# Moving one attention unit's key and query transposes from TensorE to DMA transposes, with a later second half of a weight load

## The chip, the cores and the metric

The kernel runs on one core of a Trainium2 chip. The metric is device time in microseconds (us). Three runs of the kernel before the change gave 590.16 us as their median, with 588.65 as the lowest and 591.14 as the highest. One further execution was taken with the hardware profiler; it is the one that the page and the trace tell of.

## The reference

An attention layer with normalised queries and keys, followed by a two-layer MLP with a residual. The sizes are batch 8, 12 heads, 448 positions and 64 values per head; the model width is 768 and the hidden width 3072. All inputs and the output are float32.

```python
q_n, k_n = rmsnorm(q, g_q), rmsnorm(k, g_k)            # over the 64 values of a head
scores = (1 / sqrt(64)) * matmul(q_n, k_n.transpose(0, 1, 3, 2))
attn = softmax(scores, axis=-1)
x = matmul(attn, v)                                    # (8, 12, 448, 64), then heads joined: (8, 448, 768)
xn = (x - mean(x)) / sqrt(var(x) + 1e-6) * g_ln        # over the 768 values of a row
out = x + relu(xn @ w_ch1) @ w_ch2                     # 768 -> 3072 -> 768
```

## The kernel before, in words

**Units and pairs.** The heads are taken two at a time: a pair `p` is two heads of one batch, and there are 48 pairs, six to a batch. A unit `u` is what is loaded and normalised at once: unit 4 and all later ones hold two pairs. Pairs 10 and 11 are unit 6 (the end of batch 1), pairs 12 and 13 are unit 7 (the start of batch 2), pairs 14 and 15 are unit 8, pairs 16 and 17 unit 9.

**Preparing a unit** (`pieces`). Each piece has a letter: `b` begin, `a` and `c` the squares of keys and queries (ScalarE, L254), `d` and `e` the sums of these squares (VectorE, L257), `g` the root (ScalarE, L260 and L261), `i` the product of the keys with the two gains (POOL, L271), `j` the high half of the keys in float16 (ScalarE, L279), `k` their low half, a difference (VectorE, L282), `l` the scaled queries (VectorE, L79), `m` the second copy of the queries (VectorE, L318), `z` the values, and `x`, `y`, `Y` the transposes by DMA.

**Two ways to transpose.** Scores need keys and queries with the 64 (twice 64) values on the partitions. For units below `DMA_UNIT`, TensorE transposes them against an identity matrix: `trans_k` and `trans_q` issue seven matmuls each for a pair into the PSUM bank `tr` (L360, L363, L374, L377), and VectorE copies each result to SBUF (L365, L382). From `DMA_UNIT` on, SP issues six DMA transposes for a unit (L298, L304 three times, L310 twice), straight from SBUF to SBUF; the queries are then scaled in four pieces instead of one, so that they lie in the order that these transfers want; and the values come by five cast-on-the-way DMAs that POOL issues (L212, L215) instead of a staging load and three casts on POOL (L324, L330). Keys go to `kU[0]` or `kU[1]`, queries to `qU[0]` or `qU[1]`: the DMA units use buffer `u % 2`, the TensorE units one fixed buffer, `PE_SET`.

**Banks for scores.** Scores go to two PSUM banks in turn. From the pair after the first DMA unit's first pair on, the bank `tr` is free of transposes and serves as a third one (`score_bank`).

**The order of the work.** Every engine's instruction order is the order in which the program emits them; nothing is reordered by a planner. Batch 0's attention follows a list written by hand (`ORDER`). From then on, the MLP of batch `b` is emitted in chunks, and attention steps of the following batches are put between the chunks (`run_rest`). A step is numbered `7 p + i`: the scores of pair `p`, block `i`, and the product with the values for pair `p - 1`. `EARLY` and `TRANS_AT` say at which steps the pieces of units 5 to 9 are emitted; later units follow `PLAN`. `TAIL[b]` is the number of chunks at the end of batch `b`'s MLP that have no attention step beside them: with `TAIL[0] = 11`, the steps of pairs 6 to 12 are spread over the first 34 of batch 0's 45 chunks.

**The MLP of batch 0** (`first_mlp`). It has 21 chunks of the first layer (L702, PSUM tile `psH`; three more blocks were done earlier) and 24 of the second (L712, `psC`). A chunk is six matmuls. The first 12 of these 24 chunks use the first 384 columns of W2, the last 12 the other 384. From batch 1 on, the second layer works on sums and differences of W2's quarters, which VectorE forms once (`weight_sums`, L745): its twelve differences are emitted among the last nine chunks of batch 0 and the first of batch 1, and need both halves of W2.

**W2's load** (`load_w2`, L600). POOL issues it in two halves, each one DMA that reads float32 and writes 128 x 24 x 384 float16. Half 0 is emitted at step 47, half 1 at step 61, in each case behind that step's pieces, which include `i`, the key product on POOL. A matmul that reads a half waits for the whole transfer.

**SP's queue** carries the loads of queries and keys, the DMA transposes and most stores, in program order; `RING` says at which pieces the loads of later units are emitted.

Of the kernel before, what the change touches and what calls it, by code (L numbers as in the profile page):

```python
# [22 lines left out]
UNITS = [(0, 0, 1), (0, 2, 1), (0, 4, 2), (0, 8, 2)]  # L23
# [20 lines left out]
V5.3 V5.4 V5.5 Q6 a5 i5 V5.6 T3 T4 S6.0 S6.1 S6.2 S6.3 T5 S6.4 A V6.0 V6.1 N0 V6.2 N1 V6.3  # L44
S6.5 S6.6 d5 V6.4 X0 X1 U0 N2 R Q7 X2 c5 e5 j5 g5 k5 l5 z5 U1 U2 V6.5 M m5 V6.6 L7 L8k K7
""".split()
DMA_UNIT = 8
PE_SET = (DMA_UNIT + 1) % 2
EARLY = {5: (42, 49), 6: (47, 56), 7: (61, 69), 8: (75, 83), 9: (89, 97)}
TRANS_AT = {8: (84, 85, 86), 9: (100, 102, 104)}  # L50
PLAN = ((0, "bai"), (1, "dc"), (3, "j"), (5, "k"), (6, "e"), (7, "g"), (8, "l"), (9, "m"),
        (12, "z"), (15, "x"), (16, "y"), (18, "Y"))
LOAD_AT = 3, 1
# [7 lines left out]
RS_RATIO = 4.0  # L61
HALF, HCOL = NFF // 2, DM // 2
DOWN = 10
TAIL = (11, 13, 17, 13, 17, 13, 19, 0)
FLAG_AT = (6, 30)
E_RING = 9
RING = [(u, n) for u in (4, 6, *range(DMA_UNIT, len(UNITS))) for n in "kq"]


def _rsqrt(nc, out, a, t, eps, mul=1.0):  # L70
# [5 lines left out]
def _scaled(nc, out, x, r):  # L76

    g = x.shape[1]
    nc.vector.scalar_tensor_tensor(  # L79
        out=out, in0=x, scalar=8.0,  # L80
        in1=r.unsqueeze(2).broadcast_to([x.shape[0], g, D]), op0=ALU.mult, op1=ALU.mult)
# [6 lines left out]
class _Fast:  # L88
# [95 lines left out]
    def load_unit(self, u, which=(1, 0, 2)):  # L184
        nc = self.nc
        b, hs, m = UNITS[u]
        eng = nc.sync
        hS = self.hS.rearrange("p f n -> p (f n)").bitcast(FP32)
        home = {(4, 2): (hS, 0), (5, 0): (hS, 1920), (5, 1): (hS, 2816), (5, 2): (hS, 3712),
                (6, 2): (self.free, 3840), (7, 0): (self.free, 0), (7, 1): (self.free, 896),  # L190
                (7, 2): (self.free, 1792)}
        t = self.loads.setdefault(u, [None] * 3)
        for n in which:
            if (u, n) in home:
                x, c = home[u, n]
                t[n] = x[:, c:c + 896].rearrange("p (g d) -> p g d", d=D)
            else:
                t[n] = self.p_in.tile([128, 14, D], FP32, tag="kq", name="qk"[n])
            self.load_main(eng, n, t[n][:, 0:6 * m], b, hs, 2 * m)
            self.load_left(eng, n, t[n][:, 6 * m:7 * m], b, hs, 2 * m,  # L200
                           nc.gpsimd if (u, n) == (DMA_UNIT + 1, 1) else None)

    def load_v(self, u):

# [24 lines left out]
    def pieces(self, u):  # L229
# [55 lines left out]
        def qn():  # L285
            if u < DMA_UNIT:
                _scaled(nc, c["qn"][:, :, 0], c["t"][0], c["r", 0])
                return
            x, r = c["t"][0], c["r", 0]
            x3, r3 = (y[:, 0:12].rearrange("p (h j) d -> p h j d", j=3) for y in (x, r.unsqueeze(2)))  # L290
            for j in range(3):
                _scaled(nc, c["qn"][:, 4 * j:4 * j + 4, 0], x3[:, :, j], r3[:, :, j, 0])
            _scaled(nc, c["qn"][:, 12:14, 0], x[:, 12:14], r[:, 12:14])
# [47 lines left out]
        def values():  # L341
            if u >= DMA_UNIT:
                self.load_v(u)
            elif u == 0:
                vall()
            else:
                vmain()
                vleft()
# [70 lines left out]
    def score_bank(self, p):  # L419
        self.n_scores += 1  # L420
        if p > UNIT_PAIR[DMA_UNIT] and self.n_scores % 3 == 2:
            return self.ps_tr.tile([128, 512], FP32, tag="tr", name="psS3")
# [106 lines left out]
    def attention(self):  # L529

        n, nu, nb0, done = B * NPAIR, len(UNITS), NPAIR, set(ORDER)
        todo = {}
        for u in range(4, nu):
            p, m = UNIT_PAIR[u], UNITS[u][2]
            if u == 4:
                continue
            plan = [(7 * (p - 4) + x, y) for x, y in PLAN]
            if u in EARLY:
                st, e = EARLY[u]
                names = ["bai", "d", "c", "e", "j", "gz", "k", "l", "m"]  # L540
                if u > DMA_UNIT:
                    names = ["bai", "d", "c", "j", "k", "e", "gz", "l", "m"]
                plan = [(st + (e - st) * x // 9, y) for x, y in enumerate(names)]
                if u >= DMA_UNIT:
                    plan += zip(TRANS_AT[u], "xyY")
            for at, names in plan:
                if self.late_v(u):
                    names = names.replace("z", "")
                todo.setdefault(at, []).extend(
                    self.prep_ops(u)[y] for y in names if y + str(u) not in done)  # L550
                for y in set(names) & set("kl"):
                    i = RING.index((u, "qk"[y == "k"])) + 3 if u != 5 and u != 7 else nu * 2
                    if i < len(RING):
                        todo.setdefault(at + (LOAD_AT[y == "l"] if u not in EARLY else 1), []).append(
                            lambda x=RING[i]: self.load_unit(x[0], ("qk".index(x[1]),)))
                if u in (6, 7) and "b" in names:
                    todo[at].append(lambda u=u: self.load_w2(u - 6))
        steps, mark = [], [0]

        for p in range(nb0, n + 1):  # L560
            for i in range(7):
                c = []
                if i == 0 and p < n and p % NPAIR == 0 and p > nb0:
                    c.append(lambda b=p // NPAIR: self.batch(b))
                c += todo.pop(7 * p + i, [])
                if p < n and f"S{p}.{i}" not in done and i < 6:
                    c.append(lambda p=p, i=i: self.scores(p, i))
                if p > nb0:
                    for x in {0: (), 1: (0, 1)}.get(i, (i,)):
                        if f"V{p - 1}.{x}" not in done:  # L570
                            c.append(lambda p=p, x=x: self.values(p - 1, x))
                if p < n and i == 6 and f"S{p}.6" not in done:
                    c.append(lambda p=p: self.scores(p, 6))
                if p > nb0 + 1 and i == 1 and (p - 1) % NPAIR:
                    c.append(lambda p=p: self.stats(p - 2))
                if p + 1 < UNIT_PAIR[DMA_UNIT]:
                    if i == 2 and f"K{p + 1}" not in done:
                        c.append(lambda p=p: self.trans_k(p + 1))
                    if i == 4 and f"Q{p + 1}" not in done:
                        c.append(lambda p=p: self.trans_q(p + 1))  # L580
                if p > nb0 and p % NPAIR == 0 and i == 6:
                    c.append(lambda p=p: self.stats(p - 1))
                if c:
                    steps.append(c)
            if p > nb0 and p % NPAIR == 0:
                mark.append(len(steps))
        return steps, mark
# [369 lines left out]
    def run_rest(self):  # L957
        steps, mark, upto = self.steps, self.mark, self.upto
        for b in range(B):
            tail = TAIL[b]  # L960
            chunks = list(self.mlp_chunks(b))
# [267 lines left out]
```

## Time and profile before

| What | Value |
|---|---|
| Median of three runs | 590.16 us |
| Profiled execution, its own time | 588.15 us |
| Span of the profile | 586.6 us |
| TensorE busy | 557.1 us (95%) |
| VectorE busy | 381.9 us (65%) |
| ScalarE busy | 378.7 us (65%) |
| POOL busy | 174.9 us (30%) |
| Mean granted TensorE clock | 0.998 |

The profile is one execution. Its engines are PE (TensorE matmuls), PEld (TensorE weight loads, which lie beside the matmuls), DVE (VectorE), ACT (ScalarE), POOL (GpSimd) and SP, which only issues DMAs. A line such as `98.50 1.14 PE L712 MATMUL psC<-w,hS 128*128 128x384 f16 x6` gives the start, the duration of the group to its last end, the engine, the line of the kernel, the operation, what it writes and reads, the shape and the count. Matmuls overlap each other, so the time that one takes from the next is read from the starts. A bracket at the end gives the engine's idle time ahead of the instruction and what ended it. In the rows of queues, q0 is the queue that POOL's DMAs use and q1 the one of SP; the columns are packets, MB and the time of these packets as a share of 16 engines, which can pass 100%. A row of DMA issues ends with the size and the time from issue to landing. Line numbers are those of the kernel before; in the changed kernel, lines below the constants stand three further down.

### The profile page before, as it was taken

The page shows a single profiled execution, that of the slowest core. Times are in us where ns is not written, and L with a number is a line of the kernel's source. Part 1 is how long each engine was busy: PE and PEld are TensorE (multiplying, and loading weights), DVE is VectorE, ACT ScalarE, POOL GpSimd, SP SyncE. Part 2 cuts the span into 40 slices and gives each one's busy share as a digit, 9 for nine tenths or more (in the row PEclk, how much of TensorE's full clock was granted, in tenths as well). Part 3 has the DMA queues.
Part 4 walks back from the last instruction along what each step waited for, and adds up shares of the span by engine and source line. Part 5 has one row for each costly group of instructions (what it writes and reads, how often), then busy time and mean ns, then how long its engine had stood idle before and what let it go on. Part 6 is the DMA issues. An engine that isn't in the chain of part 4 may idle for free.

```text
span 586.6 us, 13477 instructions
## 1 busy us (share of the span) xinstructions
PE 557.1 (95%) x5366; PEld 407.3 (69%) x5366; DVE 381.9 (65%) x832; ACT 378.7 (65%) x693; POOL 174.9 (30%) x196
## 2 busy tenths in 40 slices
PE   3777999999999999999999999999999999999995
PEld 1555566677677768777687768777787777777773
DVE  5898666699667586855757576854757744663434
ACT  5996887438786588647787489737787477323130
POOL 2854333303241520653141421643141400020000
PEclk9999999999999999999999999999999999999999
DMA  7999998948672796967753697958843480030201
GB/s 209 285 221 236 197 197 115 145 124 124 138 100 58 181 128 131 138 158 116 130 92 57 181 134 132 131 149 124 137 60 64 126 104 1 3 107 2 82 0 58
DMA packets 172664, 71.43 MB, mean 122 GB/s; under 512 B 132548, under 2 KB 167556, under 8 KB 172596
## 3 DMA queue, kind: packets, MB, share of 16 engines
q1 hardware_dynamic: 130100, 51.60, 41.8%
q0 software_dynamic: 41552, 18.29, 24.1%
q8 instruction: 43, 0.70, 0.5%
q10 hardware_dynamic: 944, 0.62, 0.4%
q14 instruction: 25, 0.20, 0.1%
HBM read 52.30 MB, written 11.01 MB: 108 GB/s over the span
## 4 chain that ended last, share of the span: by engine, by line
PE 78%; DVE 8%; ACT 3%; DMA 2%; issue 1%; SPq 0%; DVEq 0%; ACTq 0%
PE psH L779 30%; PE psP L802 28%; PE psS L397 7%; PE oA L450 4%; PE psH L702 3%; PE psC L712 2%; PE oB L452 2%; PE psS L403 1%; DVE w2s L745 1%; DMA q<-in_q_dram 1%; ACT E L413 1%; DVE stat L625 1%; DVE khl L282 1%; DVE ssq L257 1%; DVE x L467 1%
## 5 line engine op out<-in xcount | busy, mean ns | idle before, releaser
L413 ACT ACTIVATE E<-psS,rr_all 128x448 f16<-128x448 f32 x336 | 202.9, 634 | 41.3 <-PE psS L397 36.2
L779 PE MATMUL psH<-xnT,w 128*128 128x256 f16 (+1 forms) x2016 | 225.8, 261 | 0.0
L779 PEld LDWEIGHTS <-w 128*128 128x128 f16 x2016 | 172.7, 98 | 24.0 <-issue 4.8
L782 ACT ACTIVATE hS<-psH 128x512 f16<-128x512 f32 x150 | 90.0, 600 | 96.5 <-PE psH L779 92.1
L802 PEld LDWEIGHTS <-hS 128*128 128x128 f16 x1080 | 100.0, 98 | 57.5 <-issue 1.1
L802 PE MATMUL psP<-w,hS 128*128 128x384 f16 x672 | 126.8, 326 | 0.0
L397 PE MATMUL psS<-qU,kU 128*128 128x448 f16 x288 | 102.0, 356 | 9.4 <-ACT E L413 6.0
L450 PEld LDWEIGHTS <-E 128*128 128x128 f16 x1008 | 70.6, 98 | 37.2 <-issue 4.8
L271 POOL TENSOR_TENSOR k<-k,gprod 128x896 f32<-128x896 f32 x19 | 40.4, 2128 | 166.6 <-ACT khl L254 139.0
L785 DVE TENSOR_TENSOR hS<-hS 128x512 f16<-128x512 f16 (+1 forms) x119 | 56.8, 484 | 22.3 <-ACT hS L782 20.8
L802 PE MATMUL psP<-w2s,hS 128*128 128x384 f16 (+1 forms) x408 | 69.9, 321 | 0.0
L450 PE MATMUL oA<-v,E 128*128 128x65 f16 x864 | 66.7, 193 | 0.4 <-DVE x L467 0.4
L739 DVE SCALAR_TENSOR_TENSOR x<-psP,rs_all,x 128x384 f32<-128x384 f32 x60 | 36.4, 617 | 41.9 <-PE psP L802 41.2
L452 PE MATMUL oB<-v,E 128*128 128x65 f16 x288 | 51.8, 193 | 0.3
L813 POOL TENSOR_TENSOR x<-x,hS 128x384 f32<-128x384 f32 x21 | 23.4, 1127 | 84.4 <-ACT hS L881 83.8
L212 POOL DMA_DIRECT2D v<-in_v_dram x51 | 39.1, 781 | 8.9 <-PE oB L452 8.0
L397 PEld LDWEIGHTS <-kU 128*128 128x128 f16 x288 | 28.1, 98 | 16.8 <-issue 6.0
L465 DVE RECIPROCAL rec_all<-oA 128x6 f32<-128x6 f32 x48 | 9.2, 191 | 46.8 <-PE oA L450 46.7
L282 DVE TENSOR_TENSOR khl<-k,khl 128x896 f16<-128x896 f32 x19 | 20.7, 1091 | 25.9 <-ACT khl L279 25.9
L881 ACT ACTIVATE hS<-hS,rs_all 128x384 f32<-128x384 f32 x27 | 14.6, 604 | 33.1 <-DVE hS L785 33.1
L452 PEld LDWEIGHTS <-E 128*128 128x128 f16 x336 | 32.5, 97 | 0.4 <-DVE xl L472 0.4
L257 DVE TENSOR_REDUCE ssq<-khl 128x14 f32<-128x896 f32 (+1 forms) x24 | 25.5, 1062 | 6.0 <-ACT khl L254 5.0
(136 smaller groups left out, 601.0 us busy)
## 6 DMA issues: line engine op xcount, KB each, us to landing
k<-in_k_dram SPq DMA_DIRECT2D x19, 384.0 KB, 3.9
q<-in_q_dram SPq DMA_DIRECT2D x19, 384.0 KB, 4.2
out_dram<-x SPq DMA_DIRECT2D x14, 384.0 KB, 3.0
w<-in_moe_w_ch_dram POOLq DMA_DIRECT2D x3, 1536.0 KB, 15.0
w<-in_moe_w_ch_dram POOLq DMA_DIRECT2D x2, 2304.0 KB, 19.5
out_dram<-x POOLq DMA_DIRECT2D x9, 384.0 KB, 3.0
v<-in_v_dram POOLq DMA_DIRECT2D x51, 64.0 KB, 4.2
qU<-qn SPq DMA_TRANSPOSE x85, 2.5
```

Of the source, the lines that this page charges most:

```text
L212: nc.gpsimd.dma_start(out[:, :, j, 0:D], main[:, :, j])
L257: nc.vector.tensor_reduce(out=c["ssq"][:, n], in_=c["sq", n], axis=AX.X, op=ALU.add)
L271: (nc.vector if u in DVE_KG else nc.gpsimd).tensor_tensor(out=c["t"][1], in0=c["t"][1], in1=sh.gprod.unsqueeze(1).broadcast_to([128, g, D] ...
L397: nc.tensor.matmul(ps[0][:, 0:S], c["main"][:, ts(i, 128)], c["q"][:, ts(h, S)], start=True, stop=True)
L413: nc.scalar.activation(out=o, in_=x[:, 0:S], func=AFT.Exp, scale=self.units[u][3][:, g:g + 1], bias=EXP_BIAS)
L450: nc.tensor.matmul(oA[:, t, cs], E[:, ts(t, 128)], rhs, start=(i == 0 and t == 0), stop=(i == 6 and t == 2))
L452: nc.tensor.matmul(oB[:, cs], E[:, 320:448], rhs, start=(i == 0), stop=(i == 6))
L739: self.nc.vector.scalar_tensor_tensor(out=x, in0=ps, scalar=self.rs[:, b, t:t + 1], in1=x, op0=ALU.mult, op1=ALU.add)
L779: nc.tensor.matmul(ps[:, i], sh.w1[:, dc, ts(f + i, 128)], self.xnT[:, dc, 256 - N:256], start=(i == 0 and dc == 0), stop=(i == k - 1 and ...
L782: nc.scalar.activation(out=hT[:, f:f + k], in_=ps, func=AFT.Relu)
L785: nc.vector.tensor_tensor(out=out, in0=a, in1=c, op=op)
L802: nc.tensor.matmul(bank[x][:, c], a[:, f], w[:, f, c], start=(start and f == 0), stop=(stop and f == HALF - 1))
```

## The change

- `DMA_UNIT` goes from 8 to 7: unit 7's keys and queries are transposed by six DMAs on SP at steps 70, 71 and 73, no longer by 28 matmuls of TensorE and four copies of VectorE; its query scaling is in four pieces, and its values come by five DMAs that POOL issues. The staging load of these values is still issued on SP, though nothing reads it.
- As consequences of that constant, `PE_SET` becomes buffer 0, so the TensorE units (0 to 6) use `kU[0]` and `qU[0]`, unit 7 uses buffer 1, and unit 8 buffer 0 behind unit 6; the third score bank is used from pair 13 on instead of pair 15. `RING`, and the load of unit 9 of which POOL issues a part, are written with their old numbers, so they stay.
- The second half of W2 is issued at step 75 instead of step 61, behind unit 8's key product on POOL. The first half stays at step 47.
- Unit 8's pieces between steps 79 and 80 change places: the low half of its keys comes one place sooner and its root one later. Against unit 9's order, which the constant would give it, its query sum stands sooner.
- `TAIL[0]` goes from 11 to 13: the attention steps of pairs 6 to 12 are spread over 32 chunks.

```diff
-DMA_UNIT = 8
+DMA_UNIT = 7
 PE_SET = (DMA_UNIT + 1) % 2
 EARLY = {5: (42, 49), 6: (47, 56), 7: (61, 69), 8: (75, 83), 9: (89, 97)}
-TRANS_AT = {8: (84, 85, 86), 9: (100, 102, 104)}
+TRANS_AT = {7: (70, 71, 73), 8: (84, 85, 86), 9: (100, 102, 104)}
+NAMES = {8: ["bai", "d", "c", "e", "j", "k", "gz", "l", "m"],
+         9: ["bai", "d", "c", "j", "k", "e", "gz", "l", "m"]}
+W2_AT = 47, 75
...
-TAIL = (11, 13, 17, 13, 17, 13, 19, 0)
+TAIL = (13, 13, 17, 13, 17, 13, 19, 0)
...
-RING = [(u, n) for u in (4, 6, *range(DMA_UNIT, len(UNITS))) for n in "kq"]
+RING = [(u, n) for u in (4, 6, *range(8, len(UNITS))) for n in "kq"]
...
-                           nc.gpsimd if (u, n) == (DMA_UNIT + 1, 1) else None)
+                           nc.gpsimd if (u, n) == (9, 1) else None)
...
                 names = ["bai", "d", "c", "e", "j", "gz", "k", "l", "m"]
-                if u > DMA_UNIT:
-                    names = ["bai", "d", "c", "j", "k", "e", "gz", "l", "m"]
+                if u > 7:
+                    names = NAMES[u]
                 plan = [(st + (e - st) * x // 9, y) for x, y in enumerate(names)]
...
-                if u in (6, 7) and "b" in names:
-                    todo[at].append(lambda u=u: self.load_w2(u - 6))
+        for g, at in enumerate(W2_AT):
+            todo.setdefault(at, []).append(lambda g=g: self.load_w2(g))
```

## The prediction

> **What bounds the kernel now.** I read the page's first part, then the windows, then TensorE's order of time.
>
> ```profile
> span 586.6 us, 13477 instructions
> PE 557.1 (95%) x5366; PEld 407.3 (69%) x5366; DVE 381.9 (65%) x832; ACT 378.7 (65%) x693; POOL 174.9 (30%) x196
> ```
> ```profile
> 60.00:80.00 20.00, 18.12 (x155) 11.51 (x156) 11.46 (x19) 17.42 (x35) 8.63 (x8) 1.00 1.08 200
> 80.00:100.00 20.00, 19.69 (x194) 12.93 (x193) 13.85 (x30) 16.52 (x34) 7.23 (x10) 1.00 1.06 147
> 100.00:110.00 10.00, 10.00 (x101) 6.79 (x100) 5.60 (x14) 5.40 (x9) 0.00 (x0) 1.00 0.90 153
> 110.00:120.00 10.00, 10.00 (x70) 5.94 (x68) 9.74 (x23) 3.31 (x7) 5.54 (x6) 1.00 0.87 136
> 120.00:130.00 10.00, 10.00 (x97) 7.89 (x96) 9.93 (x15) 4.09 (x7) 0.00 (x0) 1.00 0.26 88
> 130.00:140.00 10.00, 9.57 (x96) 7.25 (x93) 9.88 (x18) 7.93 (x15) 2.38 (x2) 1.00 0.72 144
> ```
>
> The columns are the stretch, its length, the busy time of PE, PEld, DVE, ACT and POOL, the granted clock, the DMA share and GB/s. From 100 to 130 us TensorE has no idle time, so here each instruction taken from it is worth its whole interval, and each wait put into it costs its whole length. This is the stage that the change edits: first MLP of batch 0, beside the attention of batch 1.
>
> ```profile
> 91.44 0.35 PE L397 MATMUL psS<-qU,kU 128*128 128x448 f16 x1
> ...
> 98.11 0.22 PE L360 MATMUL tr<-id,khl 128*128 128x128 f16 x1
> 98.16 0.50 PE L363 MATMUL tr<-id,khl 128*128 128x128 f16 x6
> 98.50 1.14 PE L712 MATMUL psC<-w,hS 128*128 128x384 f16 x6
> ...
> 108.81 0.22 PE L374 MATMUL tr<-id,qn 128*128 128x128 f16 x1
> ...
> 109.20 1.14 PE L712 MATMUL psC<-w,hS 128*128 128x384 f16 x6
> ...
> 111.80 10.90 PE L712 MATMUL psC<-w,hS 128*128 128x384 f16 x66
> 122.53 1.47 PE L779 MATMUL psH<-xnT,w 128*128 128x256 f16 x12
> ```
>
> The last 66 matmuls of the stage take 122.53 - 111.80 = 10.73 us, 0.163 us each. A chunk of six takes 0.98 us, and the 12 chunks that use the second half of W2 take 72 x 0.163 = 11.7 us. They are the last of the stage's 45.
>
> **The change, part by part.**
>
> *Transposes off TensorE.* The four groups of seven for pairs 12 and 13 go: 28 matmuls. A group holds TensorE from 98.11 to 98.50 and from 108.81 to 109.20, 0.39 us, so 4 x 0.39 = 1.56 us are gained at most. All four lie ahead of the first use of W2's second half. VectorE loses their four copies and gets unit 7's query scaling in four pieces:
>
> ```profile
> 98.92 0.64 DVE L365 COPY kU<-tr 128x960 f16<-128x960 f16 x1
> ...
> 100.47 1.29 DVE L79 SCALAR_TENSOR_TENSOR qn<-q,rr_all 128x256 f16<-128x256 f32 x4
> 101.68 0.62 DVE L382 COPY qU<-tr 128x896 f16<-128x896 f16 x1
> ```
> ```profile
> 83.21 1.09 DVE L79 SCALAR_TENSOR_TENSOR qn<-w2s,rr_all 128x896 f16<-128x896 f32 x1
> ```
>
> That is 2 x (0.64 + 0.62) = 2.5 us less, and 1.29 - 1.09 = 0.2 us more. No TensorE wait in 100 to 130 us hangs on VectorE; at most the 0.43 us of idle time in 130 to 140 us goes. I take nothing.
>
> *Transposes on SP's queue.* Unit 7 gets six transfers like unit 8's:
>
> ```profile
> 68.84 0.61 SPq L150 DMA_DIRECT2D k<-in_k_dram  x1
> 100.58 0.39 SPq L142 DMA_DIRECT2D q<-in_q_dram  x1
> ...
> 104.27 2.00 SPq L298 DMA_TRANSPOSE kU<-khl  x1
> ...
> 111.53 2.52 SPq L310 DMA_TRANSPOSE qU<-qn  x2
> ```
>
> ```profile
> 103.94 0.35 PE L397 MATMUL psS<-qU,kU 128*128 128x448 f16 x1
> ```
>
> Unit 8's last from 104.27 to 114.05, 9.8 us. Unit 7's query is scaled by 84.3, so they end near 94. Pair 12's first score stands at 103.94 (the third ahead of pair 13's keys); it comes two chunks and two groups sooner, 103.94 - 1.95 - 0.78 = 101.2. So 7 us are to spare, and SP has nothing else between 69.45 and 100.58. They cost nothing; with that cover gone the scores would wait for them, up to 9.8 us. Unit 8's own transposes now write the buffers that pair 11's scores read, but they are issued at about 103, some 3 us after those scores.
>
> *Values by transfer.* On POOL the two casts of unit 7 go and five issues come, as unit 8 has them (95.48, three in 2.30 us). POOL is idle from the end of those casts to 93.44, so this hides; pair 12's values are used only after its scores. Unit 8's key difference one place sooner, and its root one later, move among VectorE and ScalarE work with no TensorE wait behind it: nothing. A third score bank from pair 13 on is worth nothing either, since between 100 and 130 us TensorE waits for no bank; at most it shares the 0.43 us named.
>
> *Attention packed into 32 chunks instead of 34.* ScalarE's 16.52 us in 80 to 100 becomes 16.52 x 34 / 32 = 17.6 of 20, still below full. It may add some tenths of waiting ahead of W2's first use; by the next part such a wait lies beside the transfer and costs nothing.
>
> *The second half of W2, from step 61 to step 75.* This sets my forecast.
>
> ```profile
> 78.88 1.46 POOL L600 DMA_DIRECT2D w<-in_moe_w_ch_dram  x1
> ...
> 93.44 2.08 POOL L271 TENSOR_TENSOR k<-k,gprod 128x896 f32<-128x896 f32 x1 [11.69 <-issue]
> 95.48 2.30 POOL L212 DMA_DIRECT2D v<-in_v_dram  x3
> ```
> ```profile
> w<-in_moe_w_ch_dram POOLq DMA_DIRECT2D x1, 2304.0 KB, 17.7
> ```
>
> The row of 17.7 us is the second half: from 78.88 it lands at 96.6, and it is needed at 122.53 - 11.7 = 110.8. In the changed order POOL issues it behind unit 8's key product (93.44 to 95.48), where the value loads stand now. That product waits for ScalarE's square at step 75, behind the score at 91.44. The square's place moves 1.5 chunks up (by a count in both kernels' instruction orders 22 chunks stand ahead of that score now, 20.5 then): 1.5 x 0.98 = 1.46 us sooner. So it is issued at 95.48 - 1.46 = 94.0. Its first use moves 1.56 us up: 122.53 - 1.56 - 11.7 = 109.3. That leaves 15.3 us, less than either half takes now:
>
> ```profile
> w<-in_moe_w_ch_dram POOLq DMA_DIRECT2D x1, 2304.0 KB, 21.2
> ```
>
> This is the first half, issued at 61.98 beside SP's loads. How fast it moves in company and alone is in the queues' packets, for 70 to 79 us and for 88 to 94 us:
>
> ```profile
> q0 software_dynamic: 1487, 1.14, 80.7%
> q1 hardware_dynamic: 1439, 0.86, 43.0%
> ```
> ```profile
> q0 software_dynamic: 1531, 1.17, 125.5%
> ```
>
> That is 165 packets per us beside SP's loads and 255 alone. A half is 3072 rows, so 12.0 us alone and 18.6 in company. In the new place SP's queue is busy again, with two loads and unit 8's transposes from about 100 on (rows above):
>
> ```profile
> q1 hardware_dynamic: 5448, 1.90, 66.6%
> ```
>
> These are its packets from 100 to 116 us, 341 per us against 160 in the company above. Lower end: 12.0 us alone and 2.7 us, what a small value load takes to land in this window:
>
> ```profile
> v<-in_v_dram POOLq DMA_DIRECT2D x1, 64.0 KB, 2.7
> ```
>
> So 94.0 + 14.7 = 108.7, and no stall. Upper end: 18.6 + 2.7 + 2 = 23.3 us (2 us are my allowance for that doubled number of packets), landing at 117.3, a stall of 8.0. I take 21.2, as the nearest row has the same size, the same queue and SP traffic beside it: landing at 115.2, a stall of 5.9. The wait sits in TensorE's own queue, ahead of 72 matmuls, and behind those of the next stage; nobody fills it, since the attention steps are used up one chunk before. VectorE's twelve differences of W2 wait for the same transfer, and follow it as they follow TensorE now. On POOL the third value load of unit 9 waits until it lands too, and unit 9's later value loads behind that; they are needed only at pair 16, over 20 us later.
>
> On SP the loads and transposes beside W2 slow down. Unit 8's transposes end near 118 instead of 114, and the next stage's rows are transposed behind them; that stage starts at about 127, so neither is late.
>
> *The sum.* -1.56 + 5.9 = +4.3 us: the next stage starts at 115.2 + 11.7 = 126.9 instead of 122.53, and all behind it moves along. The profiled execution takes 588.15 us; the median of the runs shown is 590.16, 2.0 above it. So 592.5 by the profile, and 594.5 as the median of runs.
>
> **The rivals** (as medians).
>
> *1. W2 still lands in time.* For it: the lower end above, and the empty queue between 94 and 98 us. Against it: the loads and transposes behind that, and that neither half took under 17.7 us. From a landing before 109.3 on, the transposes' gain is all that is left: 590.16 - 1.56 = 588.6, not slower. The Trainium skill, DMA: Bandwidth & Descriptors, "Anatomy of one DMA — SWDGE (gpsimd) path", gives 2.0 us and the bytes at 436 GB/s for such a transfer, for 2304 KB an estimate of 7.4 us, by which this rival would be the outcome; this trace disagrees, with 17.7 and 21.2 us. Between this and the forecast lies a short stall, 1 to 4.4 us, which gives 589.6 to 593.
>
> *2. The stall also costs clock.* TensorE's matmuls of one shape were slower at the start of the run:
>
> ```profile
> 15.40 0.84 PE L363 MATMUL tr<-id,khl 128*128 128x128 f16 x6
> ...
> 17.73 0.35 PE L408 MATMUL psS<-qU,kU 128*128 128x448 f16 x1
> ```
> ```profile
> 14.97 0.53 PE L397 MATMUL psS<-qU,kU 128*128 128x448 f16 x1 [1.18 <-ACT E L413]
> ```
>
> The transposes took 0.84 then and 0.50 at 98.16, a score 0.53 and then 0.35, though the granted clock reads 1.00 throughout.
>
> ```profile
> 61.27 0.36 PE L397 MATMUL psS<-qU,kU 128*128 128x448 f16 x1 [1.35 <-DVE kU L365]
> ```
>
> If a stall of some 6 us brings that state back, psC runs at about half pace until it ends. At the start it lasted from 8.6 to 17.7, which bounds the cost at 9.1 / 2 = 4.5 us: 594.5 + 0 to 4.5, or 595 to 599. TensorE's longest wait after that start is the 1.35 us of this row, so before cannot tell. The Trainium skill, TensorE: Matmul & The Clock Gate, "Part 1: The HAM clock gate", says that an idle window of about 3.4 us halves the clock until a busy one of that length; an estimate from it is 1.7 us.
>
> *3. Faster after all.* All waits of TensorE from 60 to 140 us (1.88 + 0.31 + 0.43, by the windows) and the 1.56 us together are 4.2 us. It takes seven tenths of that, and W2 in time, to pass 0.5%; no part of the change addresses the largest, the 1.35 us at 61.
>
> **How the numbers follow.** 0.5% of 590.16 is 2.95 us, about what runs of this kernel can tell from no change. Forecast (stall 4.5 to 8 us, 593.1 to 596.6): 0.47. Clock rival (596.6 to 600): 0.17. Short stall (589.6 to 593.1): 0.20. In time (588.6): 0.10. Faster than 587.2: 0.06. So faster 0.06, same 0.30, slower 0.64. The range from 588.5 to 599.0 leaves out about 0.15; the forecast's own is 593.1 to 596.6.
>
> **What the profile after would show.** A wait of TensorE at the first psC matmul of the second column half, near 109, of 4 to 8 us, put down to a transfer of W2; POOL's issue of it near 94 and a time to landing near 21 us; the next stage's psH starting near 127; no tr groups of unit 7, and no wait at pair 12's scores. The clock rival would show as psC matmuls of about twice the spacing behind the wait. A time to landing below 15.3 us would make the forecast wrong, as would a wait at pair 12's scores for unit 7's transposes.

## The result, and the profile after

The changed kernel takes 595.25 us (median of six runs, 594.92 to 595.81). The kernel before, in six runs of the same comparison, takes 589.54 us (588.65 to 591.14). The ratio is 1.0096, with a 95% interval from 1.0083 to 1.0109: slower by 5.7 us. The forecast was 594.5 us, slower.

The profiled execution of the changed kernel takes 595.81 us by its own time. TensorE's granted clock, as a mean over the run, is 0.990 where it was 0.998. The page's span and its row of the engines:

```profile
span 594.3 us, 13436 instructions
PE 559.9 (94%) x5338; PEld 407.9 (69%) x5338; DVE 379.9 (64%) x831; ACT 378.7 (64%) x693; POOL 177.3 (30%) x198
```

The windows of the same stage as before the change. The columns are the stretch, its length, the busy time of PE, PEld, DVE, ACT and POOL, the granted clock, the DMA share and GB/s:

```profile
80.00:100.00 20.00, 19.88 (x198) 13.01 (x197) 13.52 (x32) 17.57 (x35) 8.22 (x10) 1.00 0.66 92
100.00:110.00 10.00, 10.00 (x94) 6.25 (x93) 4.91 (x12) 5.97 (x10) 2.04 (x3) 1.00 1.26 215
110.00:120.00 10.00, 3.89 (x15) 1.75 (x14) 5.66 (x17) 2.25 (x5) 4.45 (x6) 0.72 1.43 177
120.00:130.00 10.00, 10.00 (x59) 5.87 (x58) 6.45 (x10) 0.00 (x0) 0.23 (x1) 0.94 1.23 201
```

Up to 110 us TensorE is busy nearly all the time at full clock. From 110 to 120 it is busy for 3.89 of 10 us, and the clock reads 0.72. TensorE's order of time in the changed kernel says what it waited for; the bracket gives the idle time ahead of the instruction and what ended it:

```profile
58.36 2.60 PE L705 MATMUL psH<-w2s,w 128*128 128x384 f16 x15
...
109.60 1.15 PE L715 MATMUL psC<-w,hS 128*128 128x384 f16 x6
116.86 13.96 PE L715 MATMUL psC<-w,hS 128*128 128x384 f16 x72 [6.11 <-DMA w<-in_moe_w_ch_dram]
130.66 1.47 PE L782 MATMUL psH<-xnT,w 128*128 128x256 f16 x12
```

TensorE stops at 110.75, when the 12 chunks that use the second half of W2 are all that is left, and goes on at 116.86. POOL's order of time, and the row of DMA issues from 90 to 118 us, show the transfer that it waits for:

```profile
94.19 2.09 POOL L274 TENSOR_TENSOR k<-k,gprod 128x896 f32<-128x896 f32 x1 [11.78 <-ACT khl L257]
96.23 1.49 POOL L603 DMA_DIRECT2D w<-in_moe_w_ch_dram  x1
...
117.34 0.74 POOL L215 DMA_DIRECT2D v<-in_v_dram  x1 [4.61 <-DMA w<-in_moe_w_ch_dram]
```
```profile
w<-in_moe_w_ch_dram POOLq DMA_DIRECT2D x1, 2304.0 KB, 20.6
```

From 96.23 it lands 20.6 us later, at 116.8. Windows of 2 us show what the wait does to the clock:

```profile
114.00:116.00 2.00, 0.00 (x0) 0.00 (x0) 1.82 (x2) 0.00 (x0) 0.00 (x0) 0.58 1.42 147
116.00:118.00 2.00, 1.14 (x4) 0.54 (x4) 0.00 (x0) 0.00 (x0) 0.66 (x1) 0.50 1.60 158
118.00:120.00 2.00, 2.00 (x7) 0.88 (x6) 0.00 (x0) 0.00 (x0) 1.06 (x3) 0.50 1.62 156
120.00:122.00 2.00, 2.00 (x10) 1.08 (x9) 0.00 (x0) 0.00 (x0) 0.23 (x1) 0.71 2.15 142
122.00:124.00 2.00, 2.00 (x15) 1.18 (x13) 0.94 (x2) 0.00 (x0) 0.00 (x0) 1.00 1.77 197
```

The clock is full until 114 (the windows ahead of these read 1.00), between three and four us into the wait, then about half until 121. Seven matmuls fit into 118 to 120 us and fifteen into 122 to 124. So the 72 matmuls take 130.66 - 116.86 = 13.8 us instead of 11.7.

**Where the 7.7 us between the two spans lie.** I cut each span at the stage's first `psH` matmul (before: 57.33, the row below) and at the first one of the next stage (122.53 and 130.66).

```profile
57.33 2.60 PE L702 MATMUL psH<-w2s,w 128*128 128x384 f16 x15
```

The opening takes 1.03 us more; nothing of the change lies there, and in the kernels below it lies anywhere from 57.43 to 58.57. The stage grows from 65.20 to 72.30, by 7.10 us: 6.11 of wait and 2.1 of half clock, less the 1.56 of the transposes, which leaves 0.45 to explain (below, in the account of the prediction). The rest of the span is 0.43 us shorter.

### The profile page after: what moved, and what is told of

Same layout as the page of the kernel before. It is cut to its first block, busy times and chain, and to the rows that moved or that the text cites. A ratio compares the mean times of both kernels' runs of the same rounds, so it can differ in the third digit from the quotient of the medians.

```text
span 594.3 us, 13436 instructions
## 1 busy us (share of the span) xinstructions
PE 559.9 (94%) x5338; PEld 407.9 (69%) x5338; DVE 379.9 (64%) x831; ACT 378.7 (64%) x693; POOL 177.3 (30%) x198
## 4 chain that ended last, share of the span: by engine, by line
PE 78%; DMA 6%; DVE 4%; ACT 3%; issue 1%; SPq 1%; POOL 0%; DVEq 0%; ACTq 0%; POOLq 0%
PE psH L782 31%; PE psP L805 27%; PE psS L400 6%; PE oA L453 4%; DMA w<-in_moe_w_ch_dram 3%; PE psH L705 3%; PE psC L715 2%; PE oB L455 1%; PE psS L406 1%; DMA q<-in_q_dram 1%; ACT E L416 1%; DMA k<-in_k_dram 1%; DVE stat L628 1%; DVE qn L82 1%; ACT hS L785 0%
## 5 line engine op out<-in xcount | busy, mean ns | idle before, releaser
L788 DVE TENSOR_TENSOR hS<-hS 128x512 f16<-128x512 f16 (+1 forms) x119 | 58.7, 500 | 22.3 <-ACT hS L785 20.8
L215 POOL DMA_DIRECT2D v<-in_v_dram x54 | 41.3, 779 | 13.4 <-PE oB L455 7.8
L715 PE MATMUL psC<-w,hS 128*128 128x384 f16 x144 | 28.5, 344 | 6.1 <-DMA w<-in_moe_w_ch_dram 6.1
```

The costliest lines, as they stand in the source:

```text
L215: nc.gpsimd.dma_start(out[:, :, j, 0:D], main[:, :, j])
L715: nc.tensor.matmul(ps, hT[:, f, ts(t, 128)], sh.w2[:, f, ts(g, HCOL)], start=(f == 0), stop=(f == NFF - 1))
L788: nc.vector.tensor_tensor(out=out, in0=a, in1=c, op=op)
```

## The experiments

Each is an edit of the changed kernel unless it is said otherwise, and is timed against the kernel before, which took 589.0 us in the comparison of the first four kernels, 589.3 in the next and 589.8 in the last.

### W2 back to step 61, the rest of the change kept

```diff
-W2_AT = 47, 75
+W2_AT = 47, 61
```

> The changed kernel with the second half of W2 back at step 61; all else as changed. Theory (W2 late is the whole loss, the other parts are a small gain): issued near 79 it lands near 100 to 103, no wait at 110; what is left is 1.56 us of transposes and up to 0.43 us of idle time behind, so 587.5 to 588.0 against 589.54. Rival (unit 7's transfers are starved beside W2, which is what the later place avoids): unit 8's transfers took 17.7 us beside W2 (104.24 to 121.90) against 9.8 without; at that pace unit 7's would end near 101.5, at about pair 12's first score, and a wait of TensorE there of 1 to 5 us would leave 589 to 593.

Measured: 592.86 us (589.90 to 594.83), ratio 1.0069 (1.005 to 1.0088). The profiled execution is the fastest of them. TensorE's wait in its order of time, SP's order of time, and the transposes' times to landing (from 80 to 104 us):

```profile
105.80 0.35 PE L400 MATMUL psS<-qU,kU 128*128 128x448 f16 x1 [2.41 <-DMA qU<-qn]
```
```profile
83.97 5.86 SPq L301 DMA_TRANSPOSE kU<-khl  x1
89.94 6.78 SPq L307 DMA_TRANSPOSE qU<-qn  x3
96.76 3.59 SPq L313 DMA_TRANSPOSE qU<-qn  x2
```
```profile
kU<-khl SPq DMA_TRANSPOSE x1, 15.5
qU<-qn SPq DMA_TRANSPOSE x5, 9.9
```

No wait for W2 is left, and the next stage starts at 125.07. But unit 7's six transposes, which the changed kernel issues from 83.75 to 92.46, now take until 100.35, and pair 12's scores wait 2.4 us for the queries. So the two parts of the change are tied: with W2 at its old step, the transposes run beside it and come late; with W2 behind them, W2 comes late. The rival came true and not the theory. The 2.4 us explain the profiled execution, whose clock reads 0.997 as a mean; the median lies 3 us above that one. In the five runs from 592.77 us up, the mean clock reads 0.992 or 0.993, much as in the changed kernel's runs (0.990 to 0.994), so a longer wait with a low clock behind it would fit there. Only one execution was traced, so how long the wait is in the others stays open.

### The kernel before, with only W2 moved to step 75

```diff
-                if u in (6, 7) and "b" in names:
-                    todo[at].append(lambda u=u: self.load_w2(u - 6))
+        for g, at in enumerate((47, 75)):
+            todo.setdefault(at, []).append(lambda g=g: self.load_w2(g))
```

> The kernel before with the second half of W2 at step 75 and nothing else changed. Theory: issued behind unit 8's key product at 95.5, 20.6 us to landing, so at 116.1; needed at 110.8: a wait of 5.3 us, and about 2.1 us of low clock behind it: 589.54 + 7.4 = 596.9, more than the whole change. Rival (the packing into 32 chunks or the transfers carry part of the loss): well below that, 592 to 595.

Measured: 596.87 us (595.89 to 597.55), ratio 1.0136 (1.0113 to 1.016). TensorE's order of time:

```profile
115.71 1.12 PE L712 MATMUL psC<-w,hS 128*128 128x384 f16 x3 [5.75 <-DMA w<-in_moe_w_ch_dram]
...
130.60 1.47 PE L779 MATMUL psH<-xnT,w 128*128 128x256 f16 x12
```

The move of W2 alone brings the stall and the low clock (0.67 from 110 to 120 us), and costs 7.8 us. All the rest of the change together is then worth 2.1 us by the distances of the two kernels to before (7.8 and 5.7), and 1.6 by their medians as they stand (596.87 and 595.25): about as much as the 28 matmuls, whose working gave 1.56.

### The wait filled with idle matmuls

Thirty-six matmuls into a bank that nobody reads are put ahead of the first one that needs W2's second half; they do no work for the output.

```diff
+            if s == 0 and g == 1 and t == 0:
+                fill = self.ps_m.tile([128, 512], FP32, tag="mlp", name="psW")
+                for _ in range(36):
+                    nc.tensor.matmul(fill[:, 0:HCOL], sh.id16, sh.w2[:, 0, 0:HCOL], start=True, stop=True)
```

> The changed kernel with 36 idle matmuls of 384 columns (5.9 us) ahead of the first matmul that uses W2's second half, into a PSUM tile that nobody reads. Theory (low granted clock after the wait is worth 13.8 - 11.7 = 2.1 us): W2 lands at the same time, the wait in front shrinks to some tenths, the granted clock stays at 1.00, the 72 matmuls take 11.7 us: 595.25 - 2.1 = 593.1. Rival (they are slow for another reason, such as transfers into SBUF at the same time): unchanged, 595.2.

Measured: 592.38 us (591.77 to 593.65), ratio 1.0061 (1.0042 to 1.008). TensorE's order of time and the window:

```profile
116.28 11.88 PE L719 MATMUL psC<-w,hS 128*128 128x384 f16 x72 [0.39 <-DMA w<-in_moe_w_ch_dram]
127.99 1.47 PE L786 MATMUL psH<-xnT,w 128*128 128x256 f16 x12
```
```profile
110.00:120.00 10.00, 9.62 (x60) 5.59 (x58) 5.02 (x14) 1.63 (x5) 3.96 (x6) 1.00 1.50 167
```

The transfer lands as late as before (20.7 us from issue), the start of the 72 matmuls lies where it lay, but the clock stays at 1.00 and they take 127.99 - 116.28 = 11.7 us. So the half clock costs 2.1 us of the changed kernel by the traces; by the distances to before (5.7 and 3.3 us) it is 2.4. Nothing differs but TensorE's being busy, so the half clock follows from the idle time and not from the transfers beside it.

### Unit 8's transposes later

```diff
-TRANS_AT = {7: (70, 71, 73), 8: (84, 85, 86), 9: (100, 102, 104)}
+TRANS_AT = {7: (70, 71, 73), 8: (91, 92, 93), 9: (100, 102, 104)}
```

> The changed kernel with unit 8's six transposes at steps 91 to 93 instead of 84 to 86, so that they stand behind batch 0's stores on SP and not beside W2. Theory (company on the 16 engines sets the time to landing): 20.6 us falls to about 17 to 18.5 (two loads of SP remain), the wait falls from 6.1 to 2.5 to 4 us. Rival (W2 takes that long whatever is beside it): 20.6 us and 6.1 us stay. Pair 14's scores may wait for the later transposes, so the whole time does not count here.

Measured in a single run: 594.05 us. TensorE's order of time:

```profile
115.37 13.29 PE L715 MATMUL psC<-w,hS 128*128 128x384 f16 x72 [5.56 <-DMA w<-in_moe_w_ch_dram]
```

W2 lands 20.0 us after its issue instead of 20.6, and the wait is 5.6 us instead of 6.1. The theory, that unit 8's transposes are what slows W2, falls. From 103 to 112 us the two loads on SP keep W2's queue company by themselves: per 3 us it moves 469, 516 and 488 packets there, and they 444, 516 and 487. That is no faster than beside the transposes (489 in the changed kernel, last section), and slower than alone (776), so company does matter; it only need not be the transposes.

### The second half in two transfers, at 61 and 75

```diff
-W2_AT = 47, 75
+W2_AT = (47, (0,)), (61, (1, 0, 12)), (75, (1, 12, 24))
...
-    def load_w2(self, g):
+    def load_w2(self, g, f0=0, f1=NFF):
...
-            out=self.sh.w2[:, :, ts(g, 384)],
-            in_=self.w2[:, ts(g, 384)].rearrange("(c p) d -> p c d", p=128))
+            out=self.sh.w2[:, f0:f1, ts(g, 384)],
+            in_=self.w2[128 * f0:128 * f1, ts(g, 384)].rearrange("(c p) d -> p c d", p=128))
```

> The changed kernel with the second half of W2 in two transfers of 12 of its 24 row blocks each: one at step 61, one at step 75. Theory (the load is too long for either place: at 61 it starves unit 7's transposes by 2.4 us of TensorE wait, at 75 it is late by 6.1 us): the first part ends near 91 and leaves unit 7's transposes the engines until about 98, the second, 1536 packets, lands near 107; no wait at either place; 589.04 - 1.56 - 0.43 = 587.0. Rival (unit 7's transposes do not reach pair 12 in time beside even half of the load): a wait of 1 to 2 us at pair 12, 588 to 589.5.

Measured: 587.50 us (585.44 to 589.24, eleven runs), ratio 0.9962 (0.9948 to 0.9976). This version is faster than both kernels, 1.8 us below before, and no wait of 1 to 2 us at pair 12, as the rival had it, appears. The row of its two parts of W2's second half, SP's order of time, and the first matmul of the next stage:

```profile
w<-in_moe_w_ch_dram POOLq DMA_DIRECT2D x2, 1152.0 KB, 12.0
```
```profile
103.69 6.73 SPq L301 DMA_TRANSPOSE kU<-khl  x1
110.53 5.29 SPq L307 DMA_TRANSPOSE qU<-qn  x3
115.87 2.52 SPq L313 DMA_TRANSPOSE qU<-qn  x2
119.11 2.54 SPq L675 DMA_TRANSPOSE xnT<-xn  x2
```
```profile
123.40 1.47 PE L782 MATMUL psH<-xnT,w 128*128 128x256 f16 x12 [1.39 <-DMA xnT<-xn]
```

The first part lands at 90.6 and holds unit 7's transposes up for some 3 us only; the second, issued at 95.79, lands at 107.8, in time for the matmuls behind 109. Neither W2 nor pair 12 is waited for. What is late next is the transposes of the next stage's rows, which stand on SP's queue behind unit 8's: 1.39 us.

### Both parts of the half at step 75

```diff
-W2_AT = (47, (0,)), (61, (1, 0, 12)), (75, (1, 12, 24))
+W2_AT = (47, (0,)), (75, (1, 0, 12)), (75, (1, 12, 24))
```

> The changed kernel with the second half of W2 in two transfers of 12 row blocks, both at step 75. Theory (the bytes and SP's packets beside them set the landing): the first part lands near 105 to 108, in time; the second stays at 116 to 117, needed two chunks later than the whole was, so a wait of about 6.1 - 1.95 = 4.2 us and 1 to 2 us of low clock: 592.5 to 593.5. Rival (the cost is one per transfer, not per byte): 595 or more.

Measured: 592.08 us (590.98 to 592.94), ratio 1.0046 (1.003 to 1.0062). TensorE's order of time:

```profile
115.75 11.42 PE L715 MATMUL psC<-w,hS 128*128 128x384 f16 x60 [3.88 <-DMA w<-in_moe_w_ch_dram]
```

Here 12 of the 72 matmuls can start on the first part, and 60 wait 3.9 us for the second; the clock falls to 0.83 only (from 110 to 120 us). So the split alone saves 3 us, by letting work start on what is there, and no cost per transfer shows, as the rival had it. The earlier issue of one part saves the rest.

### The split kernel with 34 chunks again, and with unit 8's old order

```diff
-TAIL = (13, 13, 17, 13, 17, 13, 19, 0)
+TAIL = (11, 13, 17, 13, 17, 13, 19, 0)
```

> The split at 61 and 75 with batch 0's attention spread over 34 chunks again (TAIL 11). Tells what the packing into 32 chunks is worth by itself. Theory: nothing but a later need and a later issue that move alike: within 0.8 us of the split with 32 chunks. Rival (the packing buys time for VectorE's differences of W2): 1 to 2 us slower.

Measured: 588.63 us (586.93 to 590.04), ratio 0.9984 (0.9972 to 0.9996), 1.1 us above the split kernel. That is more than the 0.8 us that the theory allowed, and at the edge of what the runs can tell apart. Its wait at the next stage's rows is the longer:

```profile
PE psH L782 <- DMA xnT<-xn: 2.6, 1, 2.6
```

The second of the two kernels takes back the order of unit 8's pieces:

```diff
-NAMES = {8: ["bai", "d", "c", "e", "j", "k", "gz", "l", "m"],
+NAMES = {8: ["bai", "d", "c", "e", "j", "gz", "k", "l", "m"],
```

> The split at 61 and 75 with unit 8's pieces in the order of the kernel before. Theory: the order of unit 8's pieces is worth nothing: within 0.6 us of the split. Rival (it frees VectorE or SP sooner): 0.6 to 1.5 us slower.

Measured: 587.43 us (586.86 to 588.57), ratio 0.997 (0.9958 to 0.9981): the same as the split kernel, by its median and its interval. The order is worth nothing that shows.

### The split kernels with unit 8's transposes behind the rows

```diff
-TRANS_AT = {7: (70, 71, 73), 8: (84, 85, 86), 9: (100, 102, 104)}
+TRANS_AT = {7: (70, 71, 73), 8: (91, 92, 93), 9: (100, 102, 104)}
```

> The kernel with the second half of W2 split over steps 61 and 75, and unit 8's transposes moved from steps 84 to 86 to steps 91 to 93, so that on SP's queue the transposes of the next stage's rows stand ahead of them. Theory (SP's queue past unit 8's transposes was the last thing late in the split kernel, with a wait of 1.4 us at the next stage's first matmul): that wait goes, the next stage starts 1.0 to 1.4 us sooner, and the ratio to the kernel before falls from 0.996 to about 0.994, 586.0 to 586.6 where before takes 589.3. Rival (the wait belonged to that one execution, as the 0.2 us of the kernel with the old order suggests): nothing measurable, 587.2 to 587.8. Against both: unit 8's transposes come late for pair 14's scores, a wait there and 588 or more.

> The same with the attention steps spread over 34 chunks again instead of 32. Theory (the packing was worth 1.1 us in the split kernels only because it moved unit 8's transposes, and the rows behind them, sooner on SP's queue): with the rows ahead, the packing is worth nothing, within 0.4 us of the other kernel of this comparison. Rival (the packing has a worth of its own, in TensorE's order): 0.8 to 1.4 us slower than the other kernel.

Measured: 587.95 us (585.71 to 590.43), ratio 0.9971 (0.9955 to 0.9987), and with 34 chunks 588.05 us (586.64 to 589.47), ratio 0.9973 (0.9961 to 0.9985). SP's order of time and TensorE's, in the one with 32 chunks:

```profile
115.04 2.57 SPq L675 DMA_TRANSPOSE xnT<-xn  x2
123.81 2.18 SPq L301 DMA_TRANSPOSE kU<-khl  x1
```
```profile
58.48 2.60 PE L705 MATMUL psH<-w2s,w 128*128 128x384 f16 x15
...
122.40 1.47 PE L782 MATMUL psH<-xnT,w 128*128 128x256 f16 x12
```

In the trace the theory's step holds: the rows' transposes come at 115, the wait is gone, and the stage is 63.92 us long, 1.6 less than the 65.48 of the split kernel (57.92 to 123.40). In the runs nothing of it shows; 0.9971 and 0.9962 lie inside each other's intervals. The rest of that span, behind 122.40, is 1.4 us longer than the split kernel's, and no wait of TensorE accounts for more than 0.6 of it. Whether the wait of 1.39 us stood only in the one execution traced (the kernel with the old order shows 0.24), or the gain is given back later, stays open. On the other question, the kernels with 32 and 34 chunks take the same time once the rows are ahead, as the theory had it. That fits SP's queue as the source of the 1.1 us above, but does not prove it: the interval of such a difference is about 1.2 us to either side. By the stages of the two traces (63.92 and 63.64 us) the packing by itself costs TensorE 0.28 us.

## Why the prediction was right, and where its sizes were off

**The bound and the place** held. The wait stands at the first matmul of the second column half, put down to W2, and all behind it moves along. W2's move alone costs 7.8 us, so it is the cause and not a companion of the other parts.

**The size of the stall** came out at 6.11 us against 5.9, by terms that partly cancel. With the opening's 1.03 us taken off, the issue stands at 95.2 and not at 94.0, the landing takes 20.6 us and not 21.2, and the need comes at 109.7 and not at 109.3: 1.2 - 0.6 - 0.4 = 0.2. The issue is the mis-sized one: the packing into 32 chunks was to bring unit 8's key product 1.46 us sooner. Measured from the stage's first `psH` matmul, W2 is issued 37.87 us behind it with 32 chunks and 38.10 with 34 (the two split kernels), so it brings 0.2. The product still waits for ScalarE's square (the POOL row above), and ScalarE's order of time in the changed kernel shows what the prediction missed:

```profile
92.78 0.49 ACT L708 ACTIVATE hS<-psH 128x384 f16<-128x384 f32 x1 [0.36 <-PE psH L705]
93.17 0.94 ACT L257 ACTIVATE khl<-k 128x896 f32<-128x896 f32 x1
```

The score at step 74, behind which the prediction placed the square, does come sooner, at 91.39, which is 90.36 with the opening's 1.03 taken off, against 91.44 before. That is 1.08 us sooner and not 1.46; the stops for ScalarE at 77 to 79 us, described below, take most of the difference. But the activation of a first-layer chunk now stands between that score and the square, and waits for TensorE. The square starts at 93.17, or 92.14, against 92.36 before.

**The clock** was the step that failed by its size. The sum put it at nothing and gave it to the second rival, between 0 and 4.5 us; it costs 2.1 us by the traces. The 4.5 us were taken from slow matmuls at the start, where the granted clock reads 1.00; here it reads 0.50, so that the two are the same state is not shown. It and the forecast's stall happened together, so the mechanism is the rival's, and the time lies in the forecast's own range, 593.1 to 596.6. The Trainium skill, TensorE: Matmul & The Clock Gate, "Part 1: The HAM clock gate", puts the fall behind an idle window of about 3.4 us; this trace agrees, with full clock to 114 and a wait that began at 110.75. The estimate worked out from it, 1.7 us, is below the measured 2.1: by the windows above (0.58 and 0.71 taken as parts at full and at half clock) the clock was low from 114.3 to 121.2, and TensorE was busy in the last 4.3 us of that.

**How the median came so close.** The forecast is 590.16 + 4.3. By the traces, the stage and what lies behind it grew by 6.11 - 1.56 + 2.1 + 0.45 - 0.43 = 6.7 us, 2.4 more than the sum. The medians differ by only 5.7, and the median of before fell by 0.6 in the larger number of runs: 2.4 - 1.0 - 0.6 = 0.8, which is what the forecast is off by. So the mechanism of the stall was right, and that the median came so near is in part luck. Where the 1.0 us between traces and medians belongs is not shown; the traced executions lie 1.4 us below the median of before and 0.6 above that of the changed kernel.

**The transposes off TensorE** were worth what they were taken for. From start to start, all `tr` matmuls of the stage take 3.12 us in the changed kernel where they took 4.69. The stage's length in the changed kernel and seven of the experiments goes by one sum: 65.20, less 1.56, plus the waits and the clock loss of that kernel. What is left over is 0.3 to 0.5 us in the kernels with 32 chunks and 0.0 to 0.2 in the two with 34 (the split ones).

| Kernel | Stage | Wait and clock loss | Left over |
|---|---|---|---|
| changed | 72.30 | 6.11 + 2.1 | 0.45 |
| W2 at 61 | 66.50 | 2.41 | 0.45 |
| wait filled | 70.33 | 0.39 + 36 x 0.163 of filling | 0.43 |
| split | 65.48 | 1.39 | 0.45 |
| split, old order | 64.32 | 0.24 | 0.44 |
| split, rows first | 63.92 | 0 | 0.28 |
| split, 34 chunks | 66.43 | 2.62 | 0.17 |
| split, 34 chunks, rows first | 63.64 | 0 | 0.00 |

The traces account for the remainder in two parts. A kernel with a wait in the table has 0.17 us more than one without. The chunk at 109.60 lasts 1.15 us by its row, but without a wait chunks follow each other every 0.98 us. The idle time in the bracket counts from the later end, so a wait costs 0.17 us more than the bracket says. The other 0.28 us are the packing's "some tenths of waiting". They show at the last block of a pair's scores, four matmuls of half height (L403, later L406), here the same ones before and after:

```profile
94.24 0.57 PE L403 MATMUL psS<-qU,kU 128*64 128x448 f16 x4
```
```profile
94.19 0.88 PE L406 MATMUL psS<-qU,kU 128*64 128x448 f16 x4
```

With 32 chunks two of the stage's three such groups stop inside for ScalarE, by 0.31 us each from start to start. The twelve matmuls take 2.13 us instead of 1.70, while the other waits for ScalarE fall from 0.61 + 0.31 to 0.77: 0.43 - 0.15 = 0.28. The prediction priced this at nothing, since it was to lie beside the transfer. But the first of these stops and the 0.77 (at 77 to 79 us) lie ahead of W2's issue at 96.23, where no transfer hides them.

**VectorE's copies, the third bank, unit 8's order** were taken at nothing. No wait names the first two. The order makes no difference in the runs. The 0.43 us by which the rest of the span is shorter after the change need neither the bank nor the copies: the kernel with only W2 moved, which keeps both as before, shows 0.37 of them as well (463.70 us behind the stage, against 464.07 before and 463.64 in the changed kernel). The other experiments lie anywhere from 462.7 to 464.4, so it may be chance.

**Unit 7's transposes on SP** are hidden in the changed kernel (83.75 to 92.46, as forecast), but the cover was named wrongly. The prediction gave 7 us to spare and an empty SP queue. W2 at step 61 takes those 7 us and 2.4 more: the room is there only because W2 was moved, and the prediction did not ask what the transposes would do beside it.

**Company on the queues.** The allowance of 2 us for unit 8's transposes beside W2 stood at the upper end only, and the taken 21.2 us did not contain it. Moving those transposes away changed the landing by 0.6 us. Packets in company and alone (below) went at the rates that the prediction read from before.

**SP and POOL behind W2.** Unit 8's transposes end at 121.90, or 120.9 on the clock of before, rather than 118; nobody waited. The value load on POOL waited 4.61 us for the landing, as forecast, and nobody waited for it. Behind them on SP, the rows for the next stage were said not to be late. That is so beside the stall, and the split kernel shows that without the stall it is the next thing late.

**The rivals.** W2 in time did not happen, and neither did the short stall; the split kernel is what the first would have looked like, 1.8 us below before where that rival had 1.56.

## What to carry to other kernels

A wait in a saturated engine costs its own length and, on TensorE, what the granted clock loses behind it if the wait is long: here 6.1 us of wait cost 8.2, a wait of 3.9 us still lowered the clock, and waits of 2.6 us and less left it at 1.00. A bulk load and a chain of small transfers slow each other, so two moves that are each hidden alone must be priced together, each beside the other's new place. Where a large transfer is needed in parts, splitting it lets one part go early and the other behind the small transfers; here that turned a loss of 5.7 us into a gain of 1.8.

## What the runs showed of the hardware

**Two queues share by packets, one for one.** From 100 to 103 us W2's queue is alone in the changed kernel, and from 106 to 109 the loads of SP are beside it. The columns are packets, MB and the packets' time as a share of 16 engines:

```profile
q0 software_dynamic: 776, 0.60, 129.9%
```
```profile
q0 software_dynamic: 523, 0.40, 85.0%
q1 hardware_dynamic: 523, 0.24, 41.4%
```

W2 falls from 259 packets per us to 174, and SP gets exactly as many. In the following 3 us it is 455 against 450, then, beside the transposes, 489 against 498. The Trainium skill, DMA: Bandwidth & Descriptors, "Queues, rings and completion order", says that an engine takes its rows in turn by packets; these counts agree. The transposes' issue shows in the changed kernel what this does to a chain of small transfers, unit 7's ahead of W2 and unit 8's beside it:

```profile
83.75 1.70 SPq L301 DMA_TRANSPOSE kU<-khl  x1
85.80 4.09 SPq L307 DMA_TRANSPOSE qU<-qn  x3
89.94 2.52 SPq L313 DMA_TRANSPOSE qU<-qn  x2
...
104.24 9.93 SPq L301 DMA_TRANSPOSE kU<-khl  x1
114.28 5.01 SPq L307 DMA_TRANSPOSE qU<-qn  x3
119.34 2.56 SPq L313 DMA_TRANSPOSE qU<-qn  x2
```

Unit 7's six take 8.7 us from the first issue to the end of the last when alone, and 16.4 beside W2 in the kernel with W2 at step 61 (83.97 to 100.35). Unit 8's take 17.7 us here beside W2, and took 9.8 before, without it.

**Idle matmuls hold the clock.** Thirty-six matmuls without use, 5.9 us of them, kept the granted clock at 1.00 through a wait that otherwise halved it, and gave back 2.1 us.
